# Chunked attention and a mixture of experts: later pieces of expert 0's matrices, and memory rows of v copied on chip

## The chip, the cores and the metric

The kernel runs on one core of one Trainium2 chip. The metric is the device time of one execution in microseconds (us). The engines are named as in the profile: PE is TensorE (matrix products and transposes), DVE is VectorE, ACT is ScalarE, POOL is GpSimd, SP is SyncE, which here only issues transfers. Transfers (DMA) issued by any of them share the core's 16 DMA engines.

## The reference

A chunked attention is followed by a mixture of experts in which each token goes to one expert. All data are 32-bit floats. Cut to what matters:

```python
# q, k, v: (4 batches, 8 heads, 768 positions, 64); mem_k, mem_v: (4, 8, 8 memory rows, 64)
for c in range(nc):                     # chunks of 32 queries
    l_start = max(0, c_start - 16)      # 16 keys to the left, 8 to the right
    r_end = min(S, c_end + 8)
    k_full = np.concatenate([mem_k, k_ctx], axis=2)
    v_full = np.concatenate([mem_v, v_ctx], axis=2)
    a = softmax(scale * q_c @ k_full.T)
    out[:, :, c_start:c_end] = a @ v_full
x = out.transpose(0, 2, 1, 3).reshape(3072, 512)
expert = argmax(x @ w_gate)             # 8 experts
for e in range(8):                      # tokens of expert e
    y = relu(x_e @ w1[e]) @ w2[e]       # w1: 512 x 1024, w2: 1024 x 512
out = gate_probability * y
```

The 8 memory rows of v are the same for every chunk of a batch.

## The kernel before

**Blocks.** The attention runs over 32 blocks of 96 queries (`QB`), eight per batch. `load_k(j)` and `load_q(j)` bring 192 rows of k or q for two blocks (384 KB), `load_v(i)` the 128 rows of v that one block sees: a run of keys, the 8 memory rows, a run of keys, so three transfers in `load_runs` (line 617). SP issues all of them, in the order in which the block loop (lines 1160 to 1205) is written. Each of SP's transfers signals one of eight semaphores in turn, and waits for the transfer eight places earlier to have landed; it also waits for PE to have read the buffer that it overwrites (three buffers of k and q, `NV` = 6 of v).

**One block on PE.** Scores of block i (line 537, tile sc), the value products of block i - 1 (tile o, with v), the transpose of finished rows (tx), now and then the logits of a group of four or five blocks, and the transposes of q and k for later blocks (line 542, tile tqk, from kn and qn). ACT takes the exponentials, DVE divides and copies.

**Routing.** Blocks form eight groups (`GROUPS`). For each group DVE finds the expert of each token, POOL adds up `seen` block by block (line 809), and PE's rank product (tile o from onehot and seen) waits for these additions. The finished rows then go to `x_dram`, sorted by expert, by one indirect transfer per block from POOL (line 867, `scatter_one`). Each of these waits for the place in PE's program where it was written (`behind`).

**Expert 0's matrices.** `fetch_w(0, 8)` makes sixteen pieces of 256 KB, eight of w1 and then eight of w2; `fetch_piece(1)` issues one of them at the end of each block from block `FIRST_W` = 14 on, so the last in block 29. In block 29 `early_load` reads back up to 256 rows of expert 0 from `x_dram` (line 944); it waits for the scatters of the first 22 blocks.

**Behind the blocks.** The first layer of expert 0 on these early rows (tile ph, from x0T and w1) and its second layer (tile py, from w2) are placed between the last steps of attention and routing; `fetch_w(1, 1)` and `fetch_piece(4)` bring expert 1's w1, a last `fetch_piece(1)` its w2. From about 171 us on the experts follow by a plan of their own, which the change does not touch.

Of the kernel before, what the change touches and what calls it, by code (L numbers as in the profile page):

```python
# [10 lines left out]
F32 = mybir.dt.float32  # L11
# [8 lines left out]
B, H, S, D = 4, 8, 768, 64  # L20
NMEM = 8
CHUNK, LEFT, RIGHT = 32, 16, 8
QB = 96
NQB = S // QB
# [40 lines left out]
WIN = 128  # L65
# [1 line left out]
KW = NQB * PER  # L67
NV, NQ = 6, 2
DENSE = 4
FIRST_W = 14  # L70
PAIRS = QB
NSB = NB // 2
XC = 640
# [34 lines left out]
def window(qb):  # L108
    return min(max(PER * qb - LEFT, 0), KW - WIN)


def column(c):

    blk, r = divmod(c, PER)
    if QB // 2 <= r < QB // 2 + NMEM:
        return "mem", r - QB // 2
    return "key", QB * blk + (r if r < QB // 2 else r - NMEM)


def runs(start, n):  # L120

    out = []
    for p in range(n):
        kind, x = column(start + p)
        if out and out[-1][1] == kind and out[-1][2] + out[-1][3] == x:
            out[-1][3] += 1
        else:
            out.append([p, kind, x, 1])
    return out
# [401 lines left out]
def ordinary(ctx, tc, q, k, v, mem_k, mem_v, moe_w_gate, moe_w1, moe_w2, out, good):  # L531

    nc = tc.nc
# [24 lines left out]
    kpool = actx.enter_context(tc.tile_pool(name="kpool", bufs=1))  # L558
# [36 lines left out]

    vs = [kpool.tile([128, H, DV], F32, name=f"v{i}") for i in range(NV)]
    for t in vs:
        nc.gpsimd.memset(t[:, :, D:], 1.0)


    onehot = cpool.tile([QB, NB, E], F32, name="onehot")
# [12 lines left out]
    st = [dict() for _ in range(NB)]  # L614
    turned, keyed = {}, {}

    def load_runs(to, i, start, n, src, mem):

        for p, kind, r, n in runs(start, n):
            ap = (mem if kind == "mem" else src)[i // NQB, :, r : r + n].rearrange("h r d -> r h d")  # L620
            nc.sync.dma_start(to[p : p + n], ap)

# [6 lines left out]
    def load_q(j):  # L629
        t = sbs[j]["qn"] = lpool.tile([PAIRS, H, 2 * D], F32, name="qn")  # L630
        nc.sync.dma_start(t, pairs(q, j))
        sbs[j]["qT"] = qTs[j % NQ]

    def load_k(j):
        b, s = divmod(j, NSB // B)
        t = sbs[j]["kn"] = lpool.tile([PAIRS + NMEM // 2, H, 2 * D], F32, name="kn")
        nc.sync.dma_start(t[0:PAIRS], pairs(k, j))
        if s == 0:
            nc.sync.dma_start(t[PAIRS:], mem_k[b].rearrange("h (p t) d -> p h (t d)", t=2))

    def load_v(i):
        st[i]["v"] = vs[i % NV]
        load_runs(st[i]["v"][:, :, 0:D], i, window(i % NQB), WIN, v, mem_v)

    def turned_heads(t, n, x, bank=None):
        if bank is None:
# [7 lines left out]
    def turn_q(m, copy=nc.scalar.copy, bank=None):  # L654
        j, x = divmod(m, 2)
        tq = turned_heads(sbs[j]["qn"], PAIRS, x, bank)
        to = sbs[j]["qT"][D * x : D * x + D, :, x].rearrange("d a (p t) -> d a p t", t=2)
        for t in range(2):
            copy(to[:, :, :, t], tq[D * t : D * t + D])  # L659
# [235 lines left out]
    def routing(n, kinds="v"):  # L895
        while work and n and work[0][0] in kinds:
            kind, f = work.pop(0)
            f()
            n -= kind != "s"

    def hold_back():

        while work and work[0][0] == "s":
            spread.append(work.pop(0)[1])

    def scatter_some(n):
        while spread and n:
            spread.pop(0)()
            n -= 1

    def need(i, f, *lists):
        if 0 <= i < NB:
            f(i)
# [157 lines left out]
    def fetch_piece(n):  # L1071
        while pieces and n:
            pieces.pop(0)()
            n -= 1
# [65 lines left out]
    with tc.manual_schedule():  # L1140
        load_k(0)
        load_q(0)
        load_k(1)
        load_q(1)
        load_k(2)
        load_v(0)
        load_v(1)
        load_q(2)
        load_v(2)

        first = [ps_o.tile([128, 512], F32, tag="o", name="o") for _ in range(2)]
        second = ps_s.tile([128, 2, 512], F32, tag="s", name="sc")
        turn_k(0)
        turn_k(1, nc.scalar.copy)
        turn_q(0, nc.vector.tensor_copy, first[0])
        turn_q(1, bank=first[1])
        turn_k(2)
        turn_k(3, nc.scalar.copy, second[:, 0])
        early_rows()
        for i in range(NB):  # L1160
            if i // 2 + 3 < NSB:
                (load_k, load_q)[i % 2](i // 2 + 3)
            need(i + 3, load_v)
            if i > 0:
                need(i + 2, turn_q)
            scores(i)
            if i == 0:
                need(i + 2, turn_q)
            scatter_some(1)
            banks = [ps_o.tile([128, 512], F32, tag="o", name="o") for _ in range(2)]  # L1170
            cur["bank"] = banks[0]
            if i <= 23:
                routing(1, "p")
            if i >= 1:
                values(i - 1, 0, banks[0])
            need(i - 2, turn_xb)
            routing(5 if i > 23 else 3)
            done = [g for g in range(len(GROUPS)) if i - 3 == GROUPS[g][1] - 1]
            late = logits(done[0], banks[1]) if done else None
            if i >= 1:  # L1180
                values(i - 1, 1, banks[1])
            if late:
                place_logits(*late)
            if i > 23:
                routing(1, "p")
            scatter_some(1)
            need(i + 4, turn_k)
            routing(6 if i > 23 else 5)
            hold_back()
            for g in done:  # L1190
                work.extend(routed(g))
            if i == FIRST_W:
                fetch_w(0, F // 128)
            if i >= FIRST_W:
                fetch_piece(1)
            if len(scatters) >= EARLY and "early" not in cur:
                cur["early"] = i
                early_count(banks[0])
            if i == 5:
                behind(  # L1200
                    nc.gpsimd.dma_start(
                        x_dram[0:TAIL].rearrange("(x p) c -> p x c", x=2), bc(zeros.bitcast(I32), 1, 2)
                    )
                )
                behind(nc.gpsimd.dma_start(x_dram[TAIL:NER], zeros[0 : NER - TAIL].bitcast(I32)))
            if i == 29:
                early_load()
                early_gather()

        do_early(1)  # L1210
        n = NB

        def bank_pair():
            banks = [ps_o.tile([128, 512], F32, tag="o", name="o") for _ in range(2)]
            cur["bank"] = banks[0]
            return banks

        banks = bank_pair()  # L1220
        values(n - 1, 0, banks[0])
        scatter_some(1)
        turn_xb(n - 2)
        late = last_logits(n - 3, banks[1])
        values(n - 1, 1, banks[1])
        scatter_some(1)
        nc.vector.tensor_copy(*late)
        routing(99, "v")
        fetch_w(1, 1)
        fetch_piece(4)  # L1230
        do_early(1)
        banks = bank_pair()
        late = last_logits(n - 2, banks[1])
        nc.vector.tensor_copy(*late)
        do_early(1)
        turn_xb(n - 1)
        scatter_some(1)
        do_early(1)
        routing(1, "p")
        routing(99, "v")  # L1240
        hold_back()
        banks = bank_pair()
        late = last_logits(n - 1, banks[1])
        nc.vector.tensor_copy(*late)
        fetch_piece(1)
        work.extend(routed(len(GROUPS) - 1))
        routing(99)
        check_sums()
        do_early(2)
        scatter_some(1)  # L1250
        routing(1, "p")
        routing(99, "v")
        hold_back()
        do_early(1)
        scatter_some(2)
        count_up()
        index = []

        def load_index(e):
            index.append(nc.tensor.value_load(cases[0:1, e : e + 1], min_val=0, max_val=len(arms_of(e)) - 1))  # L1260

        while len(early_ops) > 1:
            scatter_some(1)
            if len(early_ops) == 2:
                load_index(0)
            do_early(1)
        zeroed = end_rows(0)
        for j in scatters:
            tc.declare_no_dep(zeroed.ins, j, reason="rows behind those of the tokens")
        assert len(early_ops) == len(index) == 1 and not spread  # L1270
        rv = nc.values_load(good[0:1, 0:1], min_val=0, max_val=1)
        tc.switch_hint({mybir.EngineType.PE: index[0]}, len(arms_of(0)), "expert0")
        nc.tensor.addr_align(PAGE, 0, 0)
        do_early(1)
# [12 lines left out]
    h = mpool.tile([128, C2, 2, HALF], F32, name="h")  # L1287
# [595 lines left out]
    with tc.tile_critical(no_gpsimd_drain=True):  # L1883
        for e in range(E + 1):
# [6 lines left out]
            for a in nc.Switch(engines=[nc.tensor], index=[index[e]], n=len(arms), hint=f"expert{e}"):  # L1891
                kind, width = arms[a]
# [75 lines left out]
```

## Time and profile before

| What | Value |
|---|---|
| Time, median of 3 runs | 484.14 us (481.38 to 488.29) |
| Profiled execution: its own time | 489.62 us |
| Profiled execution: span | 487.7 us |
| PE busy, share of the span | 459.7 us, 94% |
| DVE, ACT, POOL busy | 282.2, 207.9, 146.8 us |
| Blocks (first scores to the last value products) | 10.5 to 147 us |
| Experts | from 171 us on |

A row of the page's time slices gives, for each of 40 equal slices, the busy share in tenths. In a row of the order of time the first number is the start, the second the length; in square brackets stands how long the engine had been idle and what ended it. PEclk is the clock granted to PE as a share of 2.4 GHz.

### The profile page before, as it was taken

The page shows a single profiled execution, that of the slowest core. Times are in us where ns is not written, and L with a number is a line of the kernel's source. Part 1 is how long each engine was busy: PE and PEld are TensorE (multiplying, and loading weights), DVE is VectorE, ACT ScalarE, POOL GpSimd, SP SyncE. Part 2 cuts the span into 40 slices and gives each one's busy share as a digit, 9 for nine tenths or more (in the row PEclk, how much of TensorE's full clock was granted, in tenths as well). Part 3 has the DMA queues.
Part 4 walks back from the last instruction along what each step waited for, and adds up shares of the span by engine and source line. Part 5 has one row for each costly group of instructions (what it writes and reads, how often), then busy time and mean ns, then how long its engine had stood idle before and what let it go on. Part 6 is the DMA issues. An engine that isn't in the chain of part 4 may idle for free. (4 is left out here: it accounts for less than half of the span.)

```text
span 487.7 us, 10618 instructions
## 1 busy us (share of the span) xinstructions
PE 459.7 (94%) x3944; PEld 420.6 (86%) x3944; DVE 282.2 (58%) x548; ACT 207.9 (43%) x389; POOL 146.8 (30%) x191
## 2 busy tenths in 40 slices
PE   5899999987999899999999999999999999999992
PEld 4898888877889769999999999977778999989992
DVE  4477587656255576842766667645447776365511
ACT  3677676555352126331452254243313643144212
POOL 3010224313253406623254044113230451352004
PEclk9999999999599999999999999999999999999998
DMA  9999999999977777587899194491533876600002
GB/s 199 180 207 221 237 234 235 258 215 267 247 167 204 243 227 184 133 231 185 168 288 203 46 306 99 89 286 59 102 74 91 287 163 199 154 5 27 1 1 88
DMA packets 103191, 83.06 MB, mean 170 GB/s; under 512 B 40433, under 2 KB 86094, under 8 KB 103120
## 3 DMA queue, kind: packets, MB, share of 16 engines
q1 hardware_dynamic: 94704, 67.94, 61.1%
q0 software_dynamic: 6912, 13.54, 8.7%
q8 instruction: 49, 0.80, 0.7%
q10 hardware_dynamic: 1504, 0.59, 0.5%
q14 instruction: 22, 0.18, 0.1%
HBM read 65.62 MB, written 21.28 MB: 178 GB/s over the span
## 5 line engine op out<-in xcount | busy, mean ns | idle before, releaser
L1483 POOL DMA_INDIRECT out_dram<-y,lab x42 | 49.1, 1170 | 144.3 <-ACT y L1470 30.8
L954 POOL DMA_INDIRECT lab<-x_dram,rows x42 | 52.4, 1247 | 47.9 <-PE sum_r L537 16.9
L537 PE MATMUL o<-v,ex 128*96 128x65 f32 x512 | 56.8, 256 | 0.2 <-issue 0.2
L537 PEld LDWEIGHTS o<-v,ex 128*96 128x96 f32 x512 | 50.6, 170 | 5.0 <-issue 2.3
L537 PE MATMUL sum_p<-xsT,w 128*128 128x140 f32 (+7 forms) x256 | 48.7, 336 | 3.2 <-DVE y L1472 1.5
L537 PEld LDWEIGHTS sum_p<-xsT,w 128*128 128x128 f32 x256 | 41.5, 190 | 7.5 <-DVE y L1472 2.4
L867 POOL DMA_INDIRECT x_dram<-xr,dest x32 | 29.7, 928 | 59.8 <-PE o L537 34.0
L659 ACT COPY qT<-tqk 64x384 f32<-64x384 f32 x60 | 30.1, 502 | 38.4 <-PE tqk L542 26.5
L537 PE MATMUL sum_p<-h,w 128*128 128x140 f32 (+7 forms) x256 | 45.7, 333 | 0.0
L537 PEld LDWEIGHTS sum_p<-h,w 128*128 128x128 f32 x256 | 41.5, 190 | 2.4 <-issue 0.2
L724 ACT ACTIVATE ex<-sc,cst 128x256 f32<-128x256 f32 x96 | 38.6, 472 | 10.1 <-PE sc L537 5.9
L1419 ACT COPY sum_r<-sum_p 128x640 f32<-128x640 f32 x36 | 24.4, 677 | 41.8 <-PE sum_p L537 40.4
L677 DVE COPY kT<-tqk 64x384 f32<-64x384 f32 x60 | 33.2, 554 | 11.8 <-PE tqk L542 10.7
L1437 DVE STREAM_TRANSPOSE xsT<-xs 128x1280 f32<-128x1280 f32 (+1 forms) x16 | 22.3, 1427 | 29.4 <-DMA xs<-x_dram 29.4
L537 PE MATMUL sum_r<-t,w 128*128 128x140 f32 (+5 forms) x192 | 36.8, 339 | 0.0
L537 PE MATMUL sum_p<-t,s 128*128 128x140 f32 (+5 forms) x192 | 36.7, 339 | 0.0
L537 PE MATMUL sum_q<-t,s 128*128 128x140 f32 (+5 forms) x192 | 36.5, 338 | 0.0
L738 DVE RECIPROCAL inv_all<-o 96x4 f32<-96x4 f32 x64 | 11.3, 176 | 41.4 <-PE o L537 34.9
L537 PE MATMUL sc<-qT,kT 64*64 64x96 f32 (+1 forms) x928 | 34.5, 262 | 0.3 <-issue 0.3
L537 PEld LDWEIGHTS sum_p<-t,s 128*128 128x128 f32 x192 | 31.8, 190 | 2.3
L537 PEld LDWEIGHTS sum_q<-t,s 128*128 128x128 f32 x192 | 31.8, 190 | 2.2
L537 PEld LDWEIGHTS sum_r<-t,w 128*128 128x128 f32 x192 | 31.7, 190 | 2.3
(182 smaller groups left out, 790.6 us busy)
## 6 DMA issues: line engine op xcount, KB each, us to landing
w<-in_moe_w_dram SPq DMA_DIRECT2D x28, 512.0 KB
w<-in_moe_w_dram SPq DMA_DIRECT2D x7, 2048.0 KB
xs<-x_dram SPq DMA_DIRECT2D x56, 160.0 KB
kn<-in_k_dram SPq DMA_DIRECT2D x16, 384.0 KB
qn<-in_q_dram SPq DMA_DIRECT2D x16, 384.0 KB
w<-in_moe_w_dram SPq DMA_DIRECT2D x16, 256.0 KB
x_dram<-zeros SPq DMA_DIRECT2D x8, 396.0 KB
v<-in_v_dram SPq DMA_DIRECT2D x24, 128.0 KB
```

Source lines behind the costliest of these rows:

```text
L537: i = nc.tensor.matmul(*args, **more)
L659: copy(to[:, :, :, t], tq[D * t : D * t + D])
L677: i = copy(to, of[:, :, 0:PAIRS].rearrange("d a (y z p) -> d a y z p", y=2, z=2))
L724: nc.scalar.activation(ex4[:, :, :, sl], sc4[:, :, :, sl], AF.Exp, bias=mask[:, 3 * x + g : 3 * x + g + 1], scale=D**-0.5)
L738: nc.vector.reciprocal(inv, o[:, :, D])
L867: i = nc.gpsimd.indirect_dma_start(out=x_dram, out_offset=bass.IndirectOffsetOnAxis(ap=dest[:, t : t + 1], axis=0), in_=xr[:, t % NXR].bit ...
L954: return nc.gpsimd.indirect_dma_start(out=to.bitcast(I32), out_offset=None, in_=x_dram.rearrange("r (k c) -> (r k) c", c=LB), in_offset=ba ...
L1419: op("ACT", one_op(lambda: nc.scalar.copy(to, of)), reads, writes)
L1437: op("DVE", one_op(lambda: nc.vector.transpose(to, of)), [("xs", y, a) for a in range(4)], [("x", k, 1 - y) for k in range(2)])
L1483: return nc.gpsimd.indirect_dma_start(out=out, out_offset=bass.IndirectOffsetOnAxis(ap=which.bitcast(I32), axis=0), in_=y, in_offset=None, ...
```

## The change

Three things change. `FIRST_W` goes from 14 to 22, so that blocks 22 to 31 issue ten of the sixteen pieces, and `fetch_piece(8)` behind the block loop issues the last six. The memory rows of v are loaded once per batch into a tile `mv` (`load_mem_v`, in blocks 0 to 3), and for the blocks from block 4 on that are neither the first nor the last of their batch POOL copies them into the v buffer; these are 21 blocks (4 to 6, 9 to 14, 17 to 22, 25 to 30). The other 11 blocks load them as before. The column of ones behind each head of v is set in one column instead of sixteen.

```diff
--- before.py
+++ after.py
@@ -67,7 +67,7 @@
 KW = NQB * PER
 NV, NQ = 6, 2
 DENSE = 4
-FIRST_W = 14
+FIRST_W = 22
 PAIRS = QB
 NSB = NB // 2
 XC = 640
@@ -595,7 +595,8 @@
 
     vs = [kpool.tile([128, H, DV], F32, name=f"v{i}") for i in range(NV)]
     for t in vs:
-        nc.gpsimd.memset(t[:, :, D:], 1.0)
+        nc.gpsimd.memset(t[:, :, D], 1.0)
+    mv = kpool.tile([128, H, D], F32, name="mv")
 
 
     onehot = cpool.tile([QB, NB, E], F32, name="onehot")
@@ -617,6 +618,8 @@
     def load_runs(to, i, start, n, src, mem):
 
         for p, kind, r, n in runs(start, n):
+            if kind == "mem" and mem is None:
+                continue
             ap = (mem if kind == "mem" else src)[i // NQB, :, r : r + n].rearrange("h r d -> r h d")
             nc.sync.dma_start(to[p : p + n], ap)
 
@@ -640,7 +643,15 @@
 
     def load_v(i):
         st[i]["v"] = vs[i % NV]
-        load_runs(st[i]["v"][:, :, 0:D], i, window(i % NQB), WIN, v, mem_v)
+        b, qb = divmod(i, NQB)
+        copied = i > 3 and 0 < qb < NQB - 1
+        load_runs(st[i]["v"][:, :, 0:D], i, window(qb), WIN, v, None if copied else mem_v)
+        if copied:
+            r = QB // 2 + LEFT
+            nc.gpsimd.tensor_copy(st[i]["v"][r : r + NMEM, :, 0:D], mv[32 * b : 32 * b + NMEM])
+
+    def load_mem_v(b):
+        nc.sync.dma_start(mv[32 * b : 32 * b + NMEM], mem_v[b].rearrange("h r d -> r h d"))
 
     def turned_heads(t, n, x, bank=None):
         if bank is None:
@@ -1160,6 +1171,8 @@
         for i in range(NB):
             if i // 2 + 3 < NSB:
                 (load_k, load_q)[i % 2](i // 2 + 3)
+            if i < B:
+                load_mem_v(i)
             need(i + 3, load_v)
             if i > 0:
                 need(i + 2, turn_q)
@@ -1209,6 +1222,7 @@
 
         do_early(1)
         n = NB
+        fetch_piece(8)
 
         def bank_pair():
             banks = [ps_o.tile([128, 512], F32, tag="o", name="o") for _ in range(2)]
```

**SP around block 14.** Here stand the loads that SP issues in blocks 13 to 15 (kn, qn, v as above; w is a piece). Before:

```order
L637 DMA kn<-in_k_dram 96x8x128 [waits DMAHW4_49,PE_49]
L621 DMA v_113<-in_v_dram 64x8x64 [waits DMAHW5_49,PE_49]
L621 DMA v_113<-in_mem_v_dram 8x8x64 [waits DMAHW6_49]
L621 DMA v_113<-in_v_dram 56x8x64 [waits DMAHW7_49]
L1062 DMA w_1154<-in_moe_w_dram 32x2x1024 [waits DMAHW0_49]
L631 DMA qn<-in_q_dram 96x8x128 [waits DMAHW1_49,PE_49]
L621 DMA v_108<-in_v_dram 64x8x64 [waits DMAHW2_49,PE_49]
L621 DMA v_108<-in_mem_v_dram 8x8x64 [waits DMAHW3_49]
L621 DMA v_108<-in_v_dram 56x8x64 [waits DMAHW4_49]
L1062 DMA w_1154<-in_moe_w_dram 32x2x1024 [waits DMAHW5_49]
```

Now:

```order
L640 DMA kn<-in_k_dram 96x8x128 [waits DMAHW7_49,PE_49]
L624 DMA v_113<-in_v_dram 64x8x64 [waits DMAHW0_49,PE_49]
L624 DMA v_113<-in_v_dram 56x8x64 [waits DMAHW1_49]
L634 DMA qn<-in_q_dram 96x8x128 [waits DMAHW2_49,PE_49]
L624 DMA v_108<-in_v_dram 64x8x64 [waits DMAHW3_49,PE_49]
L624 DMA v_108<-in_v_dram 56x8x64 [waits DMAHW4_49]
```

Four of ten entries are gone: two pieces and two loads of memory rows.

**SP at the end of the blocks.** The loads from the last v on (x is the early rows). Before, the two pieces at the end are those of blocks 28 and 29:

```order
L621 DMA v_109<-in_v_dram 48x8x64 [waits DMAHW3_49]
L1069 DMA w_1155<-in_moe_w_dram 128x512 [waits DMAHW4_49]
L1069 DMA w_1155<-in_moe_w_dram 128x512 [waits DMAHW5_49]
L944 DMA x_144<-x_dram 32x8x128 [waits DMASW7_49,DMAHW6_49,DMASW1_49,DMASW0_49]
...
L1062 DMA w_2456<-in_moe_w_dram 32x4x1024 [waits DMAHW2_49]
```

Now:

```order
L624 DMA v_109<-in_v_dram 48x8x64 [waits DMAHW2_49]
L1073 DMA w_1758<-in_moe_w_dram 32x2x1024 [waits DMAHW3_49]
L1073 DMA w_1758<-in_moe_w_dram 32x2x1024 [waits DMAHW4_49]
L955 DMA x_145<-x_dram 32x8x128 [waits DMASW7_49,DMAHW5_49,DMASW1_49,DMASW0_49]
...
L1080 DMA w_1759<-in_moe_w_dram 128x512 [waits DMAHW1_49]
L1080 DMA w_1759<-in_moe_w_dram 128x512 [waits DMAHW2_49]
```

The last two pieces ahead of the early rows are now the last of w1; all eight pieces of w2 follow them, ahead of expert 1's w1.

**POOL around the second group of scatters.** DMASW are the semaphores of POOL's own transfers. Before:

```order
L867 DMA x_dram<-xr,dest 6656x528 [waits DVE_49,PE_49,Pool_49]
L867 DMA x_dram<-xr,dest 6656x528 [waits PE_49] x2
L867 DMA x_dram<-xr,dest 6656x528 [waits DMASW2_49,PE_49]
L809 TENSOR_TENSOR seen<-seen,onehot 96x8 [waits DVE_49]
L809 TENSOR_TENSOR seen<-seen,onehot 96x8 [waits Pool_49] x3
```

Now:

```order
L878 DMA x_dram<-xr,dest 6656x528 [waits DVE_49,PE_49,Pool_49]
L878 DMA x_dram<-xr,dest 6656x528 [waits PE_49]
L651 COPY v_110<-mv 8x8x64 [waits DMASW7_49,DMASW0_49]
L878 DMA x_dram<-xr,dest 6656x528 [waits PE_49,Pool_49]
L878 DMA x_dram<-xr,dest 6656x528 [waits PE_49]
L820 TENSOR_TENSOR seen<-seen,onehot 96x8 [waits DVE_49]
L820 TENSOR_TENSOR seen<-seen,onehot 96x8 [waits Pool_49] x3
L651 COPY v_111<-mv 8x8x64 [waits DMASW2_49,DMAHW0_49,DMASW1_49,Pool_49]
```

The copy for block 20 stands between the second and the third scatter, and the semaphores that it waits for are those of the two scatters ahead of it; the copy for block 28 stands in the same place of the fourth group. The next copy waits for the other two scatters, behind the additions. PE's own order is unchanged.

## Rows read from the trace of the kernel before

**Rows 1.** From the page: the span, the busy times of the engines, and the slices of the granted clock of PE and of the DMA (tenths).

```profile
span 487.7 us, 10618 instructions
...
PE 459.7 (94%) x3944; PEld 420.6 (86%) x3944; DVE 282.2 (58%) x548; ACT 207.9 (43%) x389; POOL 146.8 (30%) x191
...
PEclk9999999999599999999999999999999999999998
DMA  9999999999977777587899194491533876600002
```

**Rows 2.** Windows of the blocks: start and end, length, then the busy time of PE, PE's weight loads, DVE, ACT and POOL (with counts), the granted clock, the DMA share and the rate in GB/s.

```profile
80.00:90.00 10.00, 9.91 (x191) 8.80 (x180) 7.51 (x27) 7.55 (x18) 3.32 (x9) 1.00 1.06 246
90.00:100.00 10.00, 8.30 (x134) 7.21 (x129) 7.51 (x29) 5.38 (x13) 3.69 (x8) 1.00 1.15 272
100.00:110.00 10.00, 8.49 (x148) 7.43 (x148) 4.75 (x16) 5.27 (x12) 0.99 (x2) 1.00 1.09 201
110.00:119.60 9.60, 7.47 (x124) 6.66 (x124) 6.65 (x24) 5.39 (x13) 3.65 (x8) 0.99 1.12 286
119.60:133.00 13.40, 13.34 (x138) 11.72 (x139) 4.56 (x13) 5.38 (x12) 2.78 (x3) 0.50 1.00 229
```

**Rows 3.** Waits of PE from 90 to 146 us: who waited for what, total us, times, longest.

```profile
PE tqk L542 <- DMA kn<-in_k_dram: 3.1, 3, 1.5
PE tqk L542 <- DMA qn<-in_q_dram: 1.2, 1, 1.2
PE tqk L542 <- DMA kn<-in_mem_k_dram: 0.5, 1, 0.5
```

**Rows 4.** Waits of SP's queue from 30 to 53 us, in the same columns.

```profile
SPq L621 <- PE sc L537: 5.1, 5, 1.4
SPq L637 <- PE tqk L542: 2.0, 2, 1.5
```

**Rows 5.** Order of time of SP's queue: start, length, the transfer. kn at 50.77 us is issued in block 10, at 83.74 us in block 18, at 112.53 us in block 24; w are pieces, x the early rows.

```profile
50.77 0.45 SPq L637 DMA_DIRECT2D kn<-in_k_dram  x1
...
67.19 0.44 SPq L1062 DMA_DIRECT2D w<-in_moe_w_dram  x1
...
83.74 0.56 SPq L637 DMA_DIRECT2D kn<-in_k_dram  x1
...
112.53 0.38 SPq L637 DMA_DIRECT2D kn<-in_k_dram  x1
...
130.02 1.02 SPq L1069 DMA_DIRECT2D w<-in_moe_w_dram  x2
137.29 1.81 SPq L944 DMA_DIRECT2D x<-x_dram  x4
```

**Rows 6.** Order of time of PE: sc rows are the scores that begin a block (44.80: block 9; 48.10: 10; 79.70: 18; 105.79: 24; 121.11: 27; 127.21: 28), the seen row is the rank product of the third group (blocks 10 to 13), ph and py are expert 0's early layers.

```profile
44.80 0.89 PE L537 MATMUL sc<-qT,kT 64*64 64x96 f32 x32
...
48.10 0.89 PE L537 MATMUL sc<-qT,kT 64*64 64x96 f32 x32
...
79.70 0.89 PE L537 MATMUL sc<-qT,kT 64*64 64x96 f32 x32
...
84.20 0.33 PE L537 MATMUL o<-seen,ones 96*96 96x32 f32 x2
...
105.79 0.89 PE L537 MATMUL sc<-qT,kT 64*64 64x96 f32 x32
...
119.66 0.87 PE L542 MATMUL tqk<-cst,kn 96*128 96x96 f32 x4 [1.53 <-DMA kn<-in_k_dram]
...
121.11 1.56 PE L537 MATMUL sc<-qT,kT 64*64 64x96 f32 x32
...
127.21 1.56 PE L537 MATMUL sc<-qT,kT 64*64 64x96 f32 x32
...
146.99 1.94 PE L537 MATMUL ph<-x0T,w 128*128 128x256 f32 x8
...
163.79 1.89 PE L537 MATMUL py<-w,h 128*128 128x256 f32 x8
...
171.25 0.45 PE L537 MATMUL sum_r<-nought 128*128 128x320 bf16 x2 [1.59 <-issue]
```

**Rows 7.** Issues of transfers: the pieces of expert 0, and the memory rows of v, with the size of one.

```profile
w<-in_moe_w_dram SPq DMA_DIRECT2D x16, 256.0 KB
...
v<-in_mem_v_dram SPq DMA_DIRECT2D x32, 16.0 KB
```

**Rows 8.** SP's entries for the memory rows of v: count, length in ns (least, median, most), first and last start.

```profile
L621 SPq DMA_DIRECT2D v<-in_mem_v_dram x32: 283/544/1752, 7.6 to 129.1; - x32
```

**Rows 9.** Order of time of POOL: the largest memory set of the start, three of the scatters and one group of additions on seen (75.83 is the second scatter of the second group, 134.06 the twenty-second of all).

```profile
0.74 1.41 POOL L594 MEMSET qT<- 64x768 f32 x2 [0.29 <-POOLq L1954]
...
54.90 0.94 POOL L867 DMA_INDIRECT x_dram<-xr,dest  x1 [0.30 <-issue]
...
75.83 0.93 POOL L867 DMA_INDIRECT x_dram<-xr,dest  x1 [1.79 <-PE o L537]
...
81.72 1.03 POOL L809 TENSOR_TENSOR seen<-seen,onehot 96x8 f32<-96x8 f32 x4 [1.35 <-DVE onehot L807]
...
134.06 0.92 POOL L867 DMA_INDIRECT x_dram<-xr,dest  x1 [4.05 <-PE o L537]
```

**Rows 10.** From the summary of the instructions on the tiles of labels: time from issue to landing of those of POOL's indirect transfers for which the trace has it (the stores of the experts).

```profile
DMA to landing us min/median/max: 2.8/3.6/6.1
```

## The prediction

> **What bounds the kernel now.** I read the windows first, then the waits of TensorE (PE), then the order of time on PE, SyncE (SP) and GpSimd (POOL). The page shows a PE that is nearly full from end to end and a DMA that is full for the first quarter only [rows 1]. The windows put the one weak stretch there [rows 2]: PE is busy 9.91 of 10 us from 80 to 90 us, then 8.30, 8.49 and 7.47 of 9.6 us up to 119.6, while the DMA share stays above 1. Then PE is busy all the time, but the granted clock is 0.50, the lower level of 1.2 GHz, for 13.4 us. What PE waited for in 90 to 146 us is transfers of k, q and memory keys: 3.1 + 1.2 + 0.5 = 4.8 us [rows 3]. No other wait in the attention blocks is as large. So the blocks are bound by PE up to block 20 and by late loads from there to block 26.
>
> Why the loads are late stands in the queue of SP. Before the pieces of expert 0 begin, SP has time to spare: in 30 to 53 us it waited over 7 us for PE to free a buffer [rows 4]. The first piece goes out at 67.19 us, in block 14 [rows 5]. The load of k issued in block 18 then starts 83.74 - 79.70 = 4.0 us after its block's scores, the one in block 24 112.53 - 105.79 = 6.7 us after [rows 5, 6]. The second is the load for which PE waits 1.53 us before 119.66 us [rows 6]; the first is within half a microsecond of its use (the 0.5 us wait of rows 3 is for memory keys sent right behind it). So some 4 us of lateness is the point from which PE stalls.
>
> The slow clock is the second cost. A block without logits takes 48.10 - 44.80 = 3.30 us at 2.4 GHz and 127.21 - 121.11 = 6.10 us at 1.2 GHz [rows 6], a factor of 1.85. Of 13.3 busy us in that stretch, 13.3 x (1 - 1/1.85) = 6.1 us are lost. The Trainium skill (TensorE: Matmul & The Clock Gate, HAM oscillation) prices a throttled stretch at its length times one half; this would be 6.7 us here, and the sum below would come out 0.6 us lower; the blocks show a factor of 1.85 and not its 2.
>
> **The change part by part.** *Pieces from block 22.* Sixteen pieces of 256 KB [rows 7] stood in blocks 14 to 29; now ten stand in 22 to 31 and six behind. Ahead of every k and q load from block 22 on there are eight fewer, ahead of those of blocks 15 to 21 none. A piece takes between 256 KB at 286 GB/s, 0.9 us (the rate of 110 to 119.6 us), and 256 KB at 246 GB/s, 1.1 us [rows 2]; I take 0.9, the row of the pieces themselves. Eight are 7.2 us of transfer that no longer stand ahead of the last k, which was 6.7 us late where 4 do no harm. So the 4.8 us of waits should go. What is late next is the last k and q, behind the two and three pieces of blocks 22 to 24: they start from SP's lateness without pieces, 50.77 - 48.10 = 2.7 us in block 10 [rows 5, 6], and gain up to 0.9 us per piece, so 4.5 to 5.4 us at the end. That leaves a wait of 0 to 2.4 us (nothing, or half of what there was); I take 0.6.
>
> *The slow clock.* It fell right behind three windows of 78 to 85% busy PE and the 1.53 us wait, and nowhere else after the start. Against "a pause is enough" speaks 171.25 us, where PE had paused 1.59 us and the clock stayed up [rows 1, 6]; there the work around it is of full 128-column products, in the blocks it is small tiles. I take it that a PE held up again and again lost the clock, and that without the waits it keeps it: 6.1 us, between 0 and 6.1.
>
> *Memory rows of v.* Removed from SP: 21 loads of 16 KB, added 4, so 17 fewer. They are 272 KB, about one piece, and 17 x 0.54 = 9.2 us of SP's queue [rows 7, 8]. In blocks 1 to 13 that time is covered by waits for buffers, in 14 to 24 it helps the loads above; I count nothing for it by itself. The Trainium skill (DMA: Bandwidth & Descriptors, Why a DMA increments its semaphore by 16 and not by 1) lets 8 partitions use only the lowest 8 engines, so that the relief there would be twice the mean. No row shows single engines, and by that rule the 0.6 us left above would be 0. The extra load in block 0 delays v there by one short entry of SP, hidden by four blocks of lead.
>
> *Copies on GpSimd.* 21 copies of 8 partitions x 512 elements. The trace has no such copy; the nearest row is a MEMSET of 768 elements, 0.70 us each [rows 9], so I take 0.5 us, between 0.2 (a POOL addition of 8 columns, 1.03 us for four with their gaps) and 1.0 (twice the work, for read and write). POOL is 30% busy [rows 1]; 21 x 0.5 = 10.5 us is no bound. Each copy is issued three blocks before its use, over 10 us of cover. What matters is what is queued behind it. In the order the copies of blocks 20 and 28 stand between the second and third scatter of a group, and wait for the two scatters just issued to land. Behind them stand two scatters and the additions on seen, for which PE waits with the rank product. In the first place: scatter at 75.83 us, landing 3.2 us later (134.06 to 137.29, when SP's load was released [rows 5, 9]) at the least and 6.1 at the most (stores of later stages [rows 10]). With 3.6 us, the median: copy from 79.4 to 79.9, two scatters at 0.92 + 0.30 us each [rows 9] to 82.3, additions to 83.4, the rank product is at 84.20 [rows 6]. It fits with 0.8 us. With 6.1 us it is late by 1.7 us. I take 0.2 us for each of two places, 0.4 in all, between 0 and 3.4.
>
> *Behind the blocks.* The early rows are loaded at 137.29 us, and the first layer's products on them begin at 146.99 [rows 5, 6]. In the new order these loads follow the last piece of the first matrix, so they can be late by what SP is late in block 29; half of 4 us at most. SP waited there for the scatter before, so I take 0.2 us, between 0 and 2. The six pieces of the second matrix are first read at 163.79 us, 16.8 us after the first layer begins [rows 6], and take 6 x 0.9 = 5.4 us of DMA.
>
> **The sum.** -4.8 - 6.1 + 0.6 + 0.4 + 0.2 = -9.7 us, against the profiled execution's 489.6 us: 479.9. That execution is 5.5 us above the median of the three runs, 484.1. If what it has over them is the profile's own, 484.1 - 9.7 = 474.4; if it is a longer slow stretch that the median run had less of, the runs come to the same 479.9. The runs shown spread over 6.9 us, as much as the slow clock costs, so neither can be excluded: I take the middle, **477 us**. Two per cent, about what a measurement of this kernel can tell from no change, is 9.7 us: 474.5 to 493.8.
>
> **The rivals.**
> - *The slow clock stays.* For it: PE lost the clock once with no pause as long as at 171 us, so small tiles alone may be enough; against: up to 90 us the same tiles on a full PE kept it [rows 1, 2]. Then only 4.8 - 1.2 us are won: 486.0 by the profile, 480.5 by the median, 483.
> - *GpSimd's wait takes the place of the loads' (slower).* At the copies of blocks 20 and 28 the additions on seen come after the rank product when a scatter takes over 4.4 us to land (84.20 - 1.03 - 2 x 1.22 - 0.5 - 75.83). Price: at 6.1 us of landing and copies of 1.0 us, 2.2 us in each place, 4.4; the pauses keep the clock low where it was and lower it at a second place, 6.1 more: 489.6 - 4.8 + 4.4 + 6.1 = 495.3 by the profile, 489.8 by the median, 492. For it: the DMA is full there; against: it is less full once the pieces are gone.
> - *The wait moves behind the blocks.* DMA work is only shifted, and the first layer needs all eight pieces of the first matrix, now sent in blocks 22 to 29, with the early rows behind them. If the queue is still 6 us late in block 29, most of the 4.8 us is waited for there, and the clock may fall as well: about 485. Against: SP reached its last piece at 130.02 us and then waited until 137.29 us for a scatter, so 7 us were to spare [rows 5].
>
> **How the numbers follow.** Forecast 0.60; the clock stays 0.18; GpSimd 0.10; the wait moves 0.12. The likeliest case by itself reaches from 473 to 481; the second adds 480 to 486, the fourth 483 to 487. From 470 (a piece at 1.1 us, no cost left) to 487 some 85% are held. Faster by over 2% means below 474.5, the median's end of the likeliest case: 0.4 of 0.60, so 0.25. Slower by over 2% is the upper half of the GpSimd case and a bit of the fourth: 0.06. The rest, 0.69, is within.
>
> **What would show it.** Right: in blocks 20 to 26 PE waits for kn and qn under 1 us in all; the granted clock is 1.00 from 20 us to the end of the blocks; the first product of expert 0 begins near 137 us, not 147. Wrong on GpSimd: PE waits for POOL additions at a rank product, with a copy and a late scatter ahead. Wrong on the clock: a 0.50 window though PE is over 95% busy before it. Wrong on the pieces: PE waits before the first product behind the blocks, for the early rows' turn or for w.

## The result: slower, and the profile after

The change takes 490.37 us (median of 20 runs) against 485.59 us for the kernel before (20 runs on the same chip), a ratio of 1.0089 with a 95% interval of 1.006 to 1.0118. It is slower by 0.6 to 1.2%, where 477 us were forecast with a range that ends at 487. The medians here and below are of all runs; the ratios leave out the slow ones, here five of the change's 20, one of them at 670.61 us.

Half of what was forecast happened. PE's waits from 80 to 146 us in the profile of the change (who waited for what, total us, times, longest):

```profile
PE o L537 <- DVE xr L751: 1.4, 1, 1.4
PE tqk L542 <- issue: 1.4, 2, 0.8
PE tqk L542 <- ACT w L758: 1.3, 1, 1.3
PE o L537 <- issue: 1.1, 3, 0.4
PE o L537 <- POOL seen L820: 0.7, 1, 0.7
```

The waits for kn and qn that [rows 3] held are gone. In their place stand others, one for the additions on seen among them. The windows that answer to [rows 2] (same columns), and two lines of the page that answer to [rows 1], show what came with them:

```profile
80.00:90.00 10.00, 9.29 (x162) 8.35 (x161) 6.55 (x25) 6.66 (x16) 5.01 (x11) 1.00 1.06 224
90.00:100.00 10.00, 8.11 (x128) 7.08 (x127) 6.45 (x23) 3.76 (x9) 4.99 (x10) 0.93 1.09 248
100.00:110.00 10.00, 8.48 (x82) 7.52 (x85) 4.95 (x17) 4.58 (x11) 2.15 (x5) 0.50 1.02 231
110.00:119.60 9.60, 9.60 (x137) 8.40 (x132) 3.51 (x13) 4.79 (x12) 1.86 (x2) 0.70 0.49 126
119.60:133.00 13.40, 11.98 (x185) 10.61 (x186) 8.40 (x29) 7.72 (x19) 7.27 (x13) 0.87 0.66 175
```

```profile
span 488.5 us, 10624 instructions
...
PEclk9999999957899999999999999999999999999998
```

The clock is at its lower level of 1.2 GHz for most of 98 to 116 us and again for a part of 125 to 130 us, where before it had one such stretch. GpSimd's order of time (start, length, operation, the idle time ahead of it and what ended it) shows the two places that the prediction named:

```profile
74.98 0.93 POOL L878 DMA_INDIRECT x_dram<-xr,dest  x1 [1.50 <-PE o L537]
79.98 0.62 POOL L651 COPY v<-mv 8x512 f32<-8x512 f32 x1 [4.08 <-DMA x_dram<-xr,dest]
80.88 0.93 POOL L878 DMA_INDIRECT x_dram<-xr,dest  x1 [0.28 <-PE tx L542]
82.11 0.93 POOL L878 DMA_INDIRECT x_dram<-xr,dest  x1 [0.30 <-issue]
83.10 1.03 POOL L820 TENSOR_TENSOR seen<-seen,onehot 96x8 f32<-96x8 f32 x4
...
116.52 0.93 POOL L878 DMA_INDIRECT x_dram<-xr,dest  x1 [3.63 <-PE o L537]
119.97 0.61 POOL L651 COPY v<-mv 8x512 f32<-8x512 f32 x1 [2.52 <-DMA x_dram<-xr,dest]
```

The copy stands until the scatter issued at 74.98 has landed, 79.98 - 74.98 = 5.0 us after its start; the additions begin at 83.10 where before they began at 81.72 [rows 9]. At the second place it is 3.5 us. PE's rows with a wait from 80 to 125 us, and the first product of expert 0:

```profile
83.91 0.35 PE L537 MATMUL o<-seen,ones 96*96 96x32 f32 x2 [0.68 <-POOL seen L820]
97.35 0.32 PE L537 MATMUL o<-v,ex 128*96 128x65 f32 x2 [0.34 <-issue]
98.07 0.22 PE L537 MATMUL o<-v,ex 128*96 128x65 f32 x1 [0.41 <-issue]
98.80 0.56 PE L542 MATMUL tqk<-cst,kn 96*128 96x96 f32 x2 [0.51 <-issue]
100.20 0.48 PE L542 MATMUL tqk<-cst,kn 96*128 96x96 f32 x2 [0.84 <-issue]
102.00 0.90 PE L542 MATMUL tqk<-cst,qn 96*128 96x96 f32 x4 [1.31 <-ACT w L758]
124.48 0.35 PE L537 MATMUL o<-onehot,cst 96*96 96x32 f32 x2 [1.40 <-DVE xr L751]
...
147.69 1.94 PE L537 MATMUL ph<-x0T,w 128*128 128x256 f32 x8
```

At the first place PE waits 0.68 us for seen. At the second it doesn't: the additions are over at 124.1 us, and the product that reads seen begins at 124.67. The 1.40 us there is a wait for DVE, and DVE had itself stood until the moment at which ScalarE went on too:

```profile
123.76 1.20 ACT L735 ACTIVATE ex<-sc,cst 128x256 f32<-128x256 f32 x3 [2.33 <-PE o L537]
123.79 0.18 DVE L749 RECIPROCAL inv_all<-o 96x4 f32<-96x4 f32 x1 [1.09 <-PE o L537]
```

The first product of expert 0 begins at 147.69 us, 0.7 us later than before [rows 6]: what the pieces gave is lost again by then. The pause of PE, ScalarE, DVE and SP from 97 to 102 us, in which GpSimd went on, was in no forecast; the second profile of the change below bears on it.

### The profile page after: what moved, and what is told of

The parts are those of the page before. It is cut to its first block, busy times and chain, and to the rows that moved or that the text cites. A ratio compares the mean times of both kernels' runs of the same rounds, so it can differ in the third digit from the quotient of the medians.

```text
span 488.5 us, 10624 instructions
## 1 busy us (share of the span) xinstructions
PE 460.8 (94%) x3944; PEld 422.1 (86%) x3944; DVE 282.4 (58%) x548; ACT 207.9 (43%) x389; POOL 158.6 (32%) x212
## 5 line engine op out<-in xcount | busy, mean ns | idle before, releaser
L537 PE MATMUL o<-v,ex 128*96 128x65 f32 x512 | 58.3, 258 | 0.8 <-issue 0.7
L537 PEld LDWEIGHTS o<-v,ex 128*96 128x96 f32 x512 | 51.7, 173 | 5.4 <-issue 2.5
```

What stands on the lines that cost most here:

```text
L537: i = nc.tensor.matmul(*args, **more)
```

## The experiments

Each kernel was timed in interleaved rounds with the kernel before on the same chip, whose median was 484.88 us in the first set (first four), 485.7 in the second and 485.62 in the third. All of them compute the whole function. The narrower column of ones is in all of them but the kernel before and the pieces alone; it was not tried by itself, and the first scores begin between 10.35 and 11.05 us in every profile, with it or without.

| run | median us | ratio to before, 95% interval |
|---|---|---|
| pieces_alone | 480.82 | 0.994 (0.9904 to 0.9976) |
| copies_alone | 492.36 | 1.0182 (1.0132 to 1.0232) |
| both_copies_act | 482.09 | 0.9973 (0.9935 to 1.0011) |
| both_copies_dve | 481.64 | 0.9949 (0.9911 to 0.9987) |
| copies_twice | 492.44 | 1.0163 (1.0101 to 1.0224) |
| five_by_loads | 480.07 | 0.9888 (0.985 to 0.9926) |
| change_again, one profiled run | 484.32 | none |
| before_again, one profiled run | 486.57 | none |
| two_by_loads | 481.04 | 0.9892 (0.9838 to 0.9946) |
| late_copies_act | 478.08 | 0.9845 (0.9805 to 0.9885) |
| pieces_alone_again | 480.40 | 0.9892 (0.9852 to 0.9932) |
| six_by_loads_again | 479.56 | 0.9885 (0.9842 to 0.9929) |

**The two parts apart.** The pieces alone are the kernel before with this edit:

```diff
-FIRST_W = 14
+FIRST_W = 22
...
         n = NB
+        fetch_piece(8)
```

> Expert 0's pieces from block 22 on, the last six behind the blocks; memory rows of v loaded by SP as before. Theory A (the copies on GpSimd wait for scatters to land, so the additions on seen come after the rank product and scatters pile up; the pieces by themselves do what was forecast): 476 to 481 us against some 485.5 before, no wait of PE for kn or qn between 90 and 125 us, no wait for additions on seen. Theory B (small tiles lose the clock in the late blocks whatever the loads do): 483 to 487, with a 0.50 stretch of 12 us or more although PE waits little. Theory C (the pieces, now among the last loads, starve all engines): 488 to 493, with the pause on PE, ACT and DVE near 97 to 102 us again.

The copies alone are the change without that edit (`FIRST_W = 14`, no `fetch_piece(8)`).

> Pieces from block 14 on as before; memory rows of v copied by GpSimd as in the change. Theory A: 489 to 495 us, with PE waiting for additions on seen at one or two rank products and the loads of k and q late as before. Theory B: 485 to 489. Theory C: 484 to 487, no pause of all engines near 97 us.

The parts have opposite signs, both as theory A has it: the later pieces are faster, the copies slower. The windows of the pieces alone, where [rows 2] had its weak stretch:

```profile
90.00:100.00 10.00, 10.00 (x181) 9.20 (x180) 9.18 (x35) 8.08 (x19) 3.59 (x8) 1.00 1.17 260
100.00:110.00 10.00, 9.22 (x186) 8.27 (x184) 6.30 (x22) 6.08 (x15) 3.69 (x4) 1.00 1.15 213
110.00:119.60 9.60, 9.21 (x163) 8.23 (x155) 7.38 (x24) 7.06 (x17) 3.70 (x8) 1.00 0.95 233
119.60:133.00 13.40, 13.40 (x239) 12.19 (x234) 7.96 (x35) 6.64 (x17) 5.69 (x13) 1.00 0.77 223
```

PE is busy, the clock stays at 2.4 GHz though up to 110 us the DMA is as full as before, and expert 0 begins at 133.20 us instead of 146.99. With the copies alone the two places are plain, first on GpSimd, then on PE:

```profile
74.83 0.92 POOL L878 DMA_INDIRECT x_dram<-xr,dest  x1 [1.50 <-PE o L537]
83.23 0.60 POOL L651 COPY v<-mv 8x512 f32<-8x512 f32 x1 [7.48 <-DMA x_dram<-xr,dest]
...
114.86 0.93 POOL L878 DMA_INDIRECT x_dram<-xr,dest  x1 [0.30 <-PE tqk L542]
121.95 0.61 POOL L651 COPY v<-mv 8x512 f32<-8x512 f32 x1 [6.16 <-DMA x_dram<-xr,dest]
```

```profile
87.12 0.53 PE L537 MATMUL o<-seen,ones 96*96 96x32 f32 x2 [3.82 <-POOL seen L820]
121.44 0.35 PE L537 MATMUL o<-onehot,cst 96*96 96x32 f32 x2 [0.57 <-DVE xr L751]
125.85 0.53 PE L537 MATMUL o<-seen,ones 96*96 96x32 f32 x2 [4.06 <-POOL seen L820]
```

With pieces still in the queue the scatters take 8.4 and 7.1 us to land, and PE stands 7.9 us for seen. It no longer waits for k or q, so that clause of the expectation missed. Its clock is 0.50 right behind each place:

```profile
86.00:99.00 13.00, 11.88 (x107) 10.68 (x108) 3.36 (x11) 3.16 (x7) 2.89 (x9) 0.50 1.11 230
99.00:120.00 21.00, 20.87 (x381) 19.06 (x380) 16.75 (x60) 15.27 (x36) 8.88 (x15) 0.99 1.09 262
120.00:126.00 6.00, 1.37 (x14) 1.12 (x13) 1.73 (x9) 0.91 (x3) 3.17 (x7) 0.76 1.16 206
126.00:140.00 14.00, 14.00 (x143) 12.36 (x144) 4.56 (x13) 5.36 (x12) 4.14 (x7) 0.50 0.59 159
```

**The copies on another engine.** In the change, `nc.gpsimd.tensor_copy` of the memory rows becomes `nc.scalar.copy`:

> The change, but ScalarE makes the 21 copies; in the order no copy waits for a scatter. Theory A: as pieces alone, 476 to 481 us, scatters spaced as before the change. Theory B: 483 to 487. Theory C: 488 to 493.

or `nc.vector.tensor_copy`:

> The change, but VectorE makes the 21 copies; no copy waits for a scatter. Theory A: as pieces alone, 476 to 481 us. Theory B: 483 to 487. Theory C: 488 to 493.

Both are 8 to 9 us under the change; no wait for seen is left, and the clock is 1.00 from 80 to 150 us. So GpSimd's part in the loss is certain. At 482.09 and 481.64 us they lie just above theory A's range and below B's. They are no faster than the pieces alone, and their profiles tell why: the first copy stands for the load of the memory rows (6.31 us on ScalarE, 5.87 on DVE), ahead of the engine's other work, and the clock from 20 to 30 us is 0.66 in both.

```profile
21.96 0.61 ACT L651 COPY v<-mv 8x512 f32<-8x512 f32 x1 [6.31 <-DMA mv<-in_mem_v_dram]
```

**Wait or occupancy.** Each copy of the change made twice:

```diff
-            nc.gpsimd.tensor_copy(st[i]["v"][r : r + NMEM, :, 0:D], mv[32 * b : 32 * b + NMEM])
+            for _ in range(2):
+                nc.gpsimd.tensor_copy(st[i]["v"][r : r + NMEM, :, 0:D], mv[32 * b : 32 * b + NMEM])
```

> The change, with each of GpSimd's 21 copies made twice in a row, into the same place. Two theories of the copies' cost. A, the wait: a copy stands until the scatters issued ahead of it have landed (5.0 and 3.5 us at the two places in the trace of the change), and its own 0.61 us matters little; the second copy of a pair finds the scatters landed. Then the change loses only 0.6 us more at each of the two places where the additions on seen end late, 1.2 us: 489 to 493 us. B, the time of the copies: GpSimd is too full, and 21 copies of 0.61 us (12.8 us) push its work back; then the loss against pieces alone (490.4 - 480.8 = 9.6 us) doubles: 498 to 501 us.

And the copies behind scatters (six blocks, although the label says five) given back to SP:

```diff
-        copied = i > 3 and 0 < qb < NQB - 1
+        copied = i > 3 and 0 < qb < NQB - 1 and i not in (20, 21, 22, 25, 28, 29)
```

> The change, with the memory rows of blocks 20, 21, 22, 25, 28 and 29 loaded from mem_v by SP again; these are the blocks whose copies stand behind a scatter on GpSimd in the trace of the change. The other 15 copies stay on GpSimd, behind additions or ahead of the first scatter. A, the wait: with no copy behind a scatter the additions on seen are in time, the matrix unit does not wait for seen or for the row numbers behind it, and the clock stays: 480 to 483 us, as with the pieces alone. B, the time of the copies: 15 of 21 copies remain, and so most of the loss, 9.6 x 15/21 = 6.9 us: 486 to 489 us.

21 more copies of 0.61 us cost 2 to 4 us, if anything (492.44 against 490.37, which stand on different runs of before; 3.6 by the ratios, whose intervals overlap), and 15 copies left in harmless places cost nothing that shows. Both lie in the bounds of the wait and outside those of occupancy.

**Which of the waits.** Only blocks 20 and 28 by SP, `i not in (20, 28)`:

> The change, with the memory rows of blocks 20 and 28 alone loaded from mem_v by SP; the other 19 copies stay on GpSimd. These two copies are the ones that stand between a scatter and the additions on seen at the two places; the copies of blocks 21, 22, 25 and 29 still stand behind scatters, but behind additions too. A1, the place: only a copy ahead of additions costs time, so this is as good as the kernel with six blocks by loads: 479 to 483 us, no wait of the matrix unit for seen, clock 1.00 there. A2, every copy behind a scatter costs, by the scatters that are held back behind it: a good part of the loss stays, 484 to 488 us.

```profile
79.25 0.92 POOL L878 DMA_INDIRECT x_dram<-xr,dest  x1 [1.00 <-PE tqk L542]
81.53 1.03 POOL L820 TENSOR_TENSOR seen<-seen,onehot 96x8 f32<-96x8 f32 x4 [1.35 <-DVE onehot L818]
84.85 0.60 POOL L651 COPY v<-mv 8x512 f32<-8x512 f32 x1 [2.29 <-DMA x_dram<-xr,dest]
```

The additions now wait for DVE alone, as before the change [rows 9]. The copy of block 21 still stands behind a scatter, with nothing urgent behind it. Four of the six runs take 479.23 to 481.17 us, as with six blocks by loads; in them the whole loss hangs on two copies of 16 KB. The other two took 488.42 and 488.99 us, where none of the 18 runs with six blocks by loads is above 482.13. They have no profile, so it is not shown that the copies left behind scatters never cost anything. One point missed: the clock dipped once here (0.86 from 90 to 100 us), behind a wait of 2.58 us for ScalarE at 96.76 us, in a pause like that of the change from 97 to 102 us.

**The two profiles again.** The change, profiled a second time:

> The change as it is, looked at a second time, with a profile of its own. The trace of the change has a stretch from 97 to 102 us in which all engines stand still for some microseconds with no releaser in the trace but issue and remote, and the low clock follows it. A, the wait alone: that stretch is an accident of the one profiled execution; it is gone here, the waits for seen (0.7 and 1.4 us in the first trace) are still there at both places, with one or two low stretches of the clock behind them, and the profiled time is 486 to 496 us. C, the late pieces and bunched scatters: the stretch belongs to the kernel and is there again between 95 and 105 us.

The pause from 97 to 102 us is gone, so the change doesn't bring it in every execution, and C as stated falls. That the copies have no part in such pauses is not shown: the other one, in two_by_loads, also came in a kernel with copies behind scatters. The two places are still there, now with landings of 5.6 us each and a wait for seen at both (the 1.4 us that the expectation takes from the first trace was the wait for DVE), and the clock falls at both, at 84 and at 118 us:

```profile
83.00 0.36 PE L537 MATMUL o<-seen,ones 96*96 96x32 f32 x2 [1.37 <-POOL seen L820]
...
116.81 0.36 PE L537 MATMUL o<-onehot,cst 96*96 96x32 f32 x2 [0.70 <-DVE xr L751]
118.90 0.53 PE L537 MATMUL o<-seen,ones 96*96 96x32 f32 x2 [1.74 <-DMA v<-in_v_dram]
```

```profile
83.00:95.00 12.00, 12.00 (x122) 10.69 (x126) 4.06 (x14) 3.22 (x8) 3.56 (x7) 0.57 0.72 194
112.00:119.00 7.00, 4.51 (x70) 3.92 (x69) 4.90 (x19) 3.35 (x9) 3.12 (x7) 0.92 0.95 232
119.00:130.00 11.00, 11.00 (x152) 10.01 (x152) 4.80 (x15) 5.26 (x12) 4.23 (x8) 0.74 0.46 127
```

The time, 484.32 us, missed the expected 486 to 496, and lies under all 20 runs of the change: what the same waits cost differs from one execution to the next. (The third row names a load, but the product needs seen, whose additions ran from 118.11 us.) The kernel before:

> The kernel before, looked at a second time, with a profile of its own. The first profiled execution took 489.6 us, the median is 484.1 to 485.6. If every execution pays the same, the waits for kn (3.1 us) and qn (1.2 us) and both low stretches of the clock (80 to 100 and 124 to 133 us) are there again and the profiled time is 488 to 490 us. If the waits change from one execution to the next, one of the two places goes without a wait or without the low clock here, and the profiled time is 481 to 487 us; then the first trace showed more than an average execution can give back.

It took 486.57 us. PE waits 4.0 us for kn and 0.9 us for qn, but the clock is 0.83 from 120 to 130 us only, about 3.4 us at the lower level where [rows 2] has 13.4. So the second reading holds. (The expectation speaks of a low stretch from 80 to 100 us; [rows 2] have none, and that clause tests nothing.)

**What SP's saved loads are worth.** The copies of blocks from 17 on by ScalarE (12 of 21; the expectation counts 15), the first nine by GpSimd, beside the pieces alone and the kernel with six blocks by loads, all on one chip:

```diff
-            nc.gpsimd.tensor_copy(st[i]["v"][r : r + NMEM, :, 0:D], mv[32 * b : 32 * b + NMEM])
+            copy = nc.gpsimd.tensor_copy if i < 17 else nc.scalar.copy
+            copy(st[i]["v"][r : r + NMEM, :, 0:D], mv[32 * b : 32 * b + NMEM])
```

> The change, with the copies of the blocks from 17 on (15 of 21) made by ScalarE, the first six by GpSimd, where no scatter is out yet. With all copies on ScalarE the first one stood 6.3 us for the load of the memory rows at the start of the kernel, ahead of ScalarE's other work, and the clock fell to 0.66 from 20 to 30 us; that is gone here. If SP's 21 saved loads are worth time, it shows now: 474 to 478 us, under the pieces alone by 3 us or more. If they are worth nothing, 478 to 482 us, the same as the pieces alone.

> The kernel before with the later pieces alone, a second time, to stand beside the other kernels on the same chip: 479 to 482 us, about 0.6 to 1.0% under the kernel before, as the first time (480.8 us).

> The change with the memory rows of blocks 20, 21, 22, 25, 28 and 29 by SP, a second time, beside the pieces alone on the same chip. If the 15 copies that are left on GpSimd, and the loads that SP no longer issues for them, are worth nothing either way, the two lie within 1 us of each other; if SP's saved loads are worth time, this one is 2 us or more under the pieces alone.

478.08, 480.40 and 479.56 us: within 2.3 us, with intervals that overlap. Six blocks by loads is within 1 us of the pieces alone, as it is if the saved loads are worth nothing. The version with ScalarE sits on the border of its two expectations: its slowest run, 478.69 us, is under eight of the eleven of the pieces alone, but with six runs on one chip whether it is really 2 us better stays open. It beats both kernels of this case in any event, by 1.2 to 2.0% under the one before.

## Why the prediction was wrong

- **Pieces from block 22, and the slow clock: right in the mechanism.** "So the 4.8 us of waits should go" and "without the waits it keeps it": in the pieces alone PE waits 1.1 us in all from 80 to 146 us, for no load, and the clock is 1.00. Its profiled execution took 477.97 us, 11.6 under that of before, where the three terms and the early rows summed to 4.8 + 6.1 - 0.6 - 0.2 = 10.1. The rival that the clock stays low with small tiles is refuted.
- **Copies on GpSimd: the step that failed**, the term of 0.4 us between 0 and 3.4. "With 3.6 us, the median ... It fits with 0.8 us" took the landing of a scatter from stores of later stages [rows 10] and from a scatter at the end of the blocks. Inside the blocks it took 5.0 and 3.5 us in one profile of the change, 5.6 and 5.6 in the other, and 8.4 and 7.1 in the copies alone, over the upper end of 6.1. The prediction's own condition for the slower rival was 4.4, and PE waited for seen at the five places of these three profiles where the landing took longer, and not at the one where it took 3.5. What the row at 134.06 us lacked was the state of the DMA beside it: in the trace of before the window of that landing (columns of [rows 2]) has a share of 0.28, while the first place lies where it is above 1.

```profile
134.00:137.30 3.30, 3.30 (x75) 3.00 (x77) 2.08 (x10) 2.66 (x7) 1.53 (x4) 1.00 0.28 89
```
 The copy's own time was well judged (0.61 us for 0.5).
- **Its price left the clock out.** The forecast let the step cost 0 to 3.4 us, pauses alone; the second low stretch stood only in the rival. More of the loss is clock than pauses. The second profile of the change shows it best. Its waits at the two places are 1.37 + 0.70 + 1.74 = 3.8 us. The clocks of 0.57, 0.92 and 0.74 in the windows shown for it make 10.3 + 1.1 + 5.7 = 17.1 us at the lower level; PE stood for about 1 of them, and by the factor 1.85 of [rows 6] the other 16 cost 7.4 us. The first product of expert 0 begins at 141.94 us, 8.7 later than with the pieces alone, although PE reached the first place 1.7 us sooner than there (81.27 against 82.94 us).
- **The first profile of the change is not explained by the two waits.** Of its pauses only the 0.68 us are a wait for seen, and the clock stayed up behind them. The windows from 98 to 116 us (0.53) and from 125 to 130 us (0.66) hold 16.9 + 3.4 = 20.3 us at the lower level, 2.7 of them with PE at rest; the other 17.6 cost 8.1 us. Ahead of these stretches lie the pause of 97 to 102 us, 0.34 + 0.41 + 0.51 + 0.84 + 1.31 = 3.4 us, and the wait of 1.40 us for DVE. Together 13.6 us; the first product of expert 0 comes 147.69 - 133.20 = 14.5 us later than with the pieces alone. Nearly all of this followed pauses whose cause was not found.
- **The rival that came true** was "GpSimd's wait takes the place of the loads'", at 492 us; 490.37 was measured. Its mechanism and places were right. That its price came so near is in part luck: the waits at the two places are under its 4.4 us in both profiles of the change (0.7 and 3.8 us), and in the first a pause without a known cause made up for it. Its chance of 0.10 was the error: "it is less full once the pieces are gone" is true behind 110 us, but at the first place, 75 to 80 us, the share is 1.11 without any piece in the queue.
- **The sum's base.** The middle between 479.9 and 474.4 assumed that the whole 9.7 us could come off the median. The second profile of before shows that not every execution has the long low stretch. The pieces alone take 4.1 and 5.2 us off the medians (two chips; 0.6 and 1.1% by the ratios), so that even without the copies 480.4 to 480.8 was to be had, at the upper end, 479.9, and not 477.
- **Memory rows of v and behind the blocks:** nothing for the first was right within 2.3 us. Behind the blocks no wait for the early rows appeared; the third rival did not happen.

What is not settled is why the copies wait for the scatters at all. The order shows the semaphores ahead of the prediction, and the profiles confirm the wait; the operands share no tile, and the same copies on DVE or ScalarE carry no such wait. A kernel that drops only that wait was not tried. Nor is it settled what the pauses of several engines are. The two long ones came while scatters that a copy had held back were issued one behind another (94.50 to 98.18 us in the first profile of the change, 91.88 to 94.33 in two_by_loads), but such a row of scatters passed without one in the second profile (93.85 to 97.82 us).

## What to carry to other kernels

Before work is put on a quiet engine, list what its queue holds at that point: a copy of 0.6 us that has to wait for transfers issued ahead of it costs their landing time to everything behind it, and here two of 21 such copies undid what the later pieces had won. Price the landing from the same stretch of the kernel, with the DMA as full as it is there, and price a pause of PE with the clock that may fall behind it. Take a second profile before a long low stretch of the clock is counted as recoverable in every run.

## What the runs showed of the hardware

- The same scatter (96 rows of 2112 bytes) lands later where the DMA is full: 3.2 us after its start at a share of 0.28 [rows 5, 9]; 3.5 at 0.69 and 5.0 at 1.11 in the change; 5.6 and 5.6 at 1.08 and 1.10 in its second profile; 5.8 and 6.1 at 1.19 and 1.16 in the copies made twice; 8.4 and 7.1 at 1.11 and 1.17 in the copies alone, so the share does not tell all. The two windows of the change:

```profile
75.00:80.00 5.00, 5.00 (x103) 4.50 (x102) 4.35 (x14) 4.00 (x10) 0.92 (x2) 1.00 1.11 273
116.50:120.00 3.50, 3.50 (x63) 3.15 (x62) 2.91 (x12) 2.79 (x7) 0.96 (x2) 1.00 0.69 184
```

  The Trainium skill (DMA: Bandwidth & Descriptors, Anatomy of one DMA — SWDGE (gpsimd) path) fits a transfer on this path as about 2.0 us and a term by its bytes, an estimate of 2.5 us for this scatter. The runs are all above it, up to more than three times.
- A pause alone doesn't tell whether the clock falls. In the second profile of the change it fell behind 1.37 us at 83.00 us; in the first it stayed behind 0.68 us at 83.91, and in the second profile of before it stayed behind a wait of 2.23 us at 101.91 us.
- Several engines can pause together in one execution and not in the next. In the first profile of the change ScalarE and DVE resume within 0.03 us of each other:

```profile
100.37 1.20 ACT L735 ACTIVATE ex<-sc,cst 128x256 f32<-128x256 f32 x3 [4.88 <-remote]
100.40 0.18 DVE L749 RECIPROCAL inv_all<-o 96x4 f32<-96x4 f32 x1 [3.07 <-remote]
```

The trace names only issue and remote as releasers; its cause was not found.
